# Chunk 1's keys moved into chunk 0's joins: a delta-rule attention and SiLU MLP kernel

## The chip, the cores and the metric

The kernel runs on one core of one Trainium2 chip. The metric is the device time of one execution in microseconds (us), taken as the median of several runs. Smaller is better. A profile of one execution, with its trace, goes with the runs.

## What is computed

Two blocks follow each other. The first is a delta-rule attention over 4 batches, 8 heads, 768 tokens and head size 48. Each head keeps a 48x48 state. The second block is a two-layer MLP on the attention's output, with 3072 tokens, 384 model features and 2048 hidden features.

```python
k_n = k / (np.linalg.norm(k, axis=-1, keepdims=True) + 1e-06)
for t in range(S):
    kt, vt, bt = (k_n[:, :, t], v[:, :, t], beta[:, :, t, None])
    y[:, :, t] = np.einsum('bhd,bhde->bhe', q[:, :, t], state)
    v_old = np.einsum('bhde,bhd->bhe', state, kt)
    state = state + bt[:, :, :, None] * np.einsum('bhd,bhe->bhde', kt, vt - v_old)
...
h = x @ w_in
g = h * (1.0 / (1.0 + np.exp(-h)))
return g @ w_out
```

Here x is y with its heads side by side. The attention's inputs are float32. The two weight matrices arrive in 64-bit floats and are narrowed to float32 on the chip.

## The kernel before

The 768 tokens are cut into 6 chunks of 128, and each chunk into two halves of 64. Chunk c is worked on for all 32 pairs of batch and head at once.

For the attention of a chunk the kernel does these things in turn. It loads keys, queries and values (`load_k`, `load_q`, `load_v`). It transposes them on the matmul engine (`turn`, L507) and copies them out with ScalarE or VectorE. It multiplies keys with keys and with queries (`score`, L536). Keys' own products go through DRAM (`block_out`, `block_in`), so that all 32x32 blocks lie side by side; VectorE then inverts them in 31 rank-one steps (`invert`, L643 and L648). The blocks are joined to the inverse of a half by small matmuls: in chunk 0 by four stages (`joins`: first, second, third, fourth, L746 to L787), in later chunks by `merge` (L821). With the inverse, `keys` (L846), `inner` (L858), `old` (L924), `update` (L878) and `new` (L937) carry the state from half to half and make the outputs. The outputs of even heads are copied into `xT` by ScalarE or VectorE (L551, L554), fourteen copies for a half; those of odd heads are copied as a whole (`part`) and then moved into `xT` by DMAs (`move`, L917).

The MLP of a half takes `hidden` (L1059: 8 pairs of feature tiles, which the text calls features 0 to 7, each in two steps of 3 matmuls, with a Silu on ScalarE at L1069 behind it) and then the second matrix: `project` (L1094) for both halves of chunk 0, `combine` (L1166) for all others. `hidden` of feature f reads piece f of `w_in`.

The weights come as eight pieces each of `w_in` and `w_out` (`fetch_w_in`, `fetch_w_out`). Each is narrowed (`narrow`) by two instructions on ScalarE (L224, L225), two on VectorE (L229, L233) and one on GpSimd (L237). `begin_next` issues the ScalarE part of the next piece, `fill` the rest in three steps.

Every engine takes its instructions in the order in which the program issues them; `pin` writes this order out. So does `in_line` for the DMAs that SyncE issues, and `linked` makes the next DMA wait until the one before it has landed. `busy` issues a matmul that only keeps the matmul engine at work.

The order around the change is written by hand. First comes straight code for chunk 0, up to the joins of its first half. Then a string of words is read by `script`: `s` is the next step of chunk 0's or 1's `solve`, `r` the next step of the MLP (`run`), `j` of the second half's joins, `p` of chunk 1's scores (`prepare`), `l` of chunk 1's and `m` of chunk 2's key lengths (`lengths`), `i` of the inversion of chunk 1's blocks, `f` and `b` are `fill` and `begin_next`, `q` turns a batch of chunk 1's queries, `g` makes the step sizes, `c` runs what is left of the MLP of chunk 0. A number behind a letter repeats the step.

Of the kernel before, what the change touches and what calls it, by code (L numbers as in the profile page):

```python
# [19 lines left out]
def kernel(  # L20
# [10 lines left out]
    nc = tc.nc  # L31
# [76 lines left out]
    def together(*parts):  # L108
        for _ in zip_longest(*parts):
            pass  # L110
# [109 lines left out]
    def narrow(to, raw):  # L220

        low, high = raw[..., 0], raw[..., 1]
        bits = to.bitcast(U32)
        pin(nc.scalar.activation(out=to, in_=high.bitcast(FP32), func=ACTF.Abs, scale=2.0**-112))  # L224
        pin(nc.scalar.activation(  # L225
            out=low.bitcast(I32), in_=low, func=ACTF.Identity, scale=2.0**-29, bias=plus23[:]
        ))
        yield
        yield pin(nc.vector.tensor_scalar(  # L229
            out=bits, in0=bits, scalar1=3, scalar2=0x7FFFFFFF,  # L230
            op0=ALU.logical_shift_left, op1=ALU.bitwise_and,
        ))
# [40 lines left out]

    def fetch_w_in(i):
        if i in (0, 1, 6):
            raw = mlp.tile([P, SIZE], U32, name="raw", tag="gT", bufs=3)[:]
# [100 lines left out]
    def square(c, b):  # L377

        if b == 0:
            sums[c] = small.tile([P, BH], FP32, name="ss", bufs=1)[:]  # L380
        if c > 2:
            squared[c, b] = zbuf[:, b].rearrange("p s a w -> p (s a) w")[:, :, 0:D]
        elif b % HB == 0:
            tag = "g" if c > 0 or b > 0 else "x"
            both = work.tile([P, HB, H, D], FP32, name="sq", tag=tag, bufs=1)
            for u in range(HB):
                squared[c, b + u] = both[:, u]
        kb = kbufs[c % 2][:, b].rearrange("p a e w -> p (a e) w")[:, :, 0:D]
        pin(nc.gpsimd.tensor_tensor(out=squared[c, b], in0=kb, in1=kb, op=ALU.mult))
# [168 lines left out]

    blocks = {}

    def dram_blocks(c):
        return tc.dram_tile([P, T, T], FP32, name=f"blocks{c}")

    def block_room(c):

# [18 lines left out]

    def block_out(c, g):

        there, ap = blocks[c][0], aps[c, g][0]
# [99 lines left out]
    def invert_first(step):  # L687
# [25 lines left out]
        def widen(to, of, q, by):  # L713
# [3 lines left out]
            else:  # L717
                pin(nc.vector.tensor_scalar(out=to, in0=of, scalar1=scale, scalar2=None, op0=ALU.mult))

        pin(nc.vector.transpose(  # L720
            out=turned[:, 0].rearrange("p n s -> p s n"), in_=x2.rearrange("p i s t -> p s i t")
        ))
        for q, by in enumerate(("dve", "dve", "act", "act")):
            widen(et, turned[:, 0], q, by)
        pin(nc.vector.transpose(
# [145 lines left out]
    def update(c, g, hf):  # L871

        if c == NCH - 1 and hf == 1:
            return
        pu = bank(CC, "pu")
        for u, p, e, n, of, _ in of_heads():
            rows = on(e, hf, g)
            yield pin(nc.tensor.matmul(  # L878
                pu[of, n * D : (n + 1) * D], lhsT=kbufs[c % 2][rows, g * HB + u, p, e, 0:D],
                rhs=zbuf[rows, g * HB + u, hf, p, 0:D], start=True, stop=True,  # L880
            ))
        to = states[g][:, :, :, 0:D]
        pin(nc.vector.tensor_tensor(out=to, in0=to, in1=by_heads(pu), op=ALU.add))
# [106 lines left out]
    def solve(c):  # L990

        if c == 0:
            together(inner(0, 0, 0, CC))
            together(inner(0, 1, 0, M))
            yield
            first_outputs(0)
            yield
            first_outputs(1)
            yield
            together(update(0, 0, 0), update(0, 1, 0))  # L1000
            yield
            together(keys(0, 0, 1), keys(0, 1, 1))
            yield
            together(inner(0, 0, 1), old(0, 0, 1))
            yield
            together(inner(0, 1, 1), old(0, 1, 1))
            yield
            together(update(0, 0, 1), update(0, 1, 1))
            yield
            together(new(0, 0, 1), new(0, 1, 1))  # L1010
            copy_out()
            copy_out()
            move()
            yield
            return
        together(merge(c, 0, False), merge(c, 1, False))
        yield
        together(keys(c, 0, 0), keys(c, 1, 0))
        yield
        together(merge(c, 0, True), merge(c, 1, True))  # L1020
        yield
        for hf in range(2):
            if hf == 1:
                together(keys(c, 0, 1), keys(c, 1, 1))
                if c > 1:
# [12 lines left out]
            move()  # L1038
            if hf == 0:
                yield  # L1040
# [192 lines left out]

    class Piece:
        def __init__(self, *name):
            self.name, self.steps, self.done = name, None, 0

        def begin(self):
            if self.steps is None:
                kind, i = self.name  # L1240
                self.steps = (narrow_w_in if kind == "in" else narrow_w_out)(i)
                next(self.steps)

    def begin(*names):
        for piece in queue:
# [7 lines left out]
            piece.begin()  # L1253
        soon.clear()

    def begin_next():
        for piece in queue:
            if piece.steps is None:
                piece.begin()
                return  # L1260

    def fill(n):
# [76 lines left out]
        pass  # L1339
    for g in range(2):  # L1340
        above_blocks(g)
    fetch_w_in(0)
    load_k(1)
    fetch_w_in(1)
    load_v(0)
    for c in range(1, NCH):
        beta_of(c)
    busy(1)
    for b in range(2, B):
        first_queries(b)  # L1350
        busy(1)
    linked(fetch_w_in, 2)
    linked(load_q, 1)
    fetch_w_in(3)
    linked(fetch_w_in, 4)
    linked(fetch_w_in, 5)
    linked(fetch_w_in, 6)
    begin(("in", 0))
    inv = invert_first(step)

# [5 lines left out]

    for n in range(1 + Q):
        done = next(inv)
        if n in (9, 11, 15, 16):
            busy(1 + n // 16, done, Sync)  # L1370
        if n in (10, 12):
            for b in range(n - 10, n - 8):
                turn(1, b, 0, M)
    stages = next(inv)

    def joins(hf, between=()):
# [15 lines left out]
    def none():  # L1392
        pass

    together(joins(0, [sized, none, none, filled(3)]))

    pieces = chained(hidden(0, 0), hidden(0, 1), project())

# [24 lines left out]
    def prepare(c):  # L1423
# [14 lines left out]
        if in_blocks(c):  # L1438
# [14 lines left out]
            block_in(c)  # L1453
            yield
            return
        block_room(1)
        for b in range(B):
            score(1, b, (0,), (CC, CC), evacuate)
            if b % HB == 1:
                block_out(1, b // HB)  # L1460
            yield
        block_in(1)
        yield
        for b in range(B):
# [13 lines left out]
    def script(text):  # L1478

        nonlocal pieces  # L1480
        for word in text.split():
# [18 lines left out]
                turn(1, queries_1.pop(0), 1, M)  # L1500
            elif what == "b":
                begin_next()
            elif what == "p":
                go(ready, n)
            elif what == "w":
# [24 lines left out]
                pieces = chained(feed_forward(1, 0), feed_forward(1, 1))  # L1530

    for text in (
        "s a a s q s b q f3 b j34 r f3 j34 r q f j34 r f2 q j38 W7 f r f b r f2 e r f h w2 f r l f s f l r2 w3 l p r l f p l s l f r l r l3 p l s l3 p l2 r l f l4 f l f l3 p l s l2 s2 f r v f r p l3 g i p f l p f i p f l i r3 i r i2 r3 i2 r i r i3 b r2 f2 r3 i r i2 r2 i f b i4 f r f r2 f r3 f i2 r f i f r3 f r f i f r i2 r i2 k i2 b r2 i r i r z r i r s r b z s b r2 t r2 f s r2 t2 m2 t2 b m f r m s f b r m r m2 b m f s r s m4 c s m7 r t s m r m5 s r m m t t",
    ):
        script(text)
    for c in range(1, NCH):
# [59 lines left out]
```

## Time and profile before

| | |
|---|---|
| median of 3 runs | 658.51 us (657.32 to 658.62) |
| profiled execution | 656.42 us, of which span 654.5 us |
| mean granted TensorE clock | 0.989 |
| TensorE matmuls (PE) busy | 630.7 us, 96% of the span |
| VectorE (DVE) busy | 395.6 us, 60% |
| ScalarE (ACT) busy | 218.9 us, 33% |
| GpSimd (POOL) busy | 89.6 us, 14% |

PE stands for TensorE's matmuls, DVE for VectorE, ACT for ScalarE, POOL for GpSimd and SP for SyncE. The profile divides the span in 40 slices of 16.4 us and gives the busy share of each engine in tenths. Its chain of waits goes back from the last instruction to what released each one. The trace also lists each engine's instructions in order of time: start in us, length in us, engine, line, operation, tiles, how often, and in brackets how long the engine was idle before and what ended it. L-numbers are lines of the kernel before.

### The profile page before, as it was taken

Reading aid. Unit: us, or ns where it says so; the run is one execution under the profiler, and the core shown is the slowest. Engines: PE = TensorE matmul, PEld = TensorE weight load, DVE = VectorE, ACT = ScalarE, POOL = GpSimd, SP = SyncE. Lnnn points to the kernel's source line nnn. Section 1 sums busy time; section 2 is a strip of 40 time slices with the busy share of each in tenths; the row PEclk is TensorE's granted clock in tenths of the full one; section 3 lists DMA queues with packets and bytes.
Section 4 is the critical chain, followed back from the end, with each engine's and each line's share of the span. In section 5 each row is a group of like instructions: output and inputs, shape, how many; then the busy total and the mean of one; then the engine's idle time right before and its main releaser. Section 6 shows DMA issues by size and latency. Waiting matters only on the chain.

```text
span 654.5 us, 20661 instructions
## 1 busy us (share of the span) xinstructions
PE 630.7 (96%) x9044; PEld 550.3 (84%) x9044; DVE 395.6 (60%) x895; ACT 218.9 (33%) x509; POOL 89.6 (14%) x94
## 2 busy tenths in 40 slices
PE   7799989999999999999999999999999999999997
PEld 5487778666789988989988989988989988889997
DVE  6846679988774985453986453986454974103112
ACT  2557763332351122451122451122451122441111
POOL 5023631335010020010020010020002000000000
PEclk9699999999999998999999999999999999999999
DMA  9976634350279333269325279325173023100101
GB/s 135 208 165 193 201 71 103 98 97 3 65 148 150 59 77 41 52 130 148 54 75 57 47 134 145 59 75 58 27 150 74 7 67 60 40 13 1 25 0 25
DMA packets 145673, 54.65 MB, mean 83 GB/s; under 512 B 117152, under 2 KB 138912, under 8 KB 145584
## 3 DMA queue, kind: packets, MB, share of 16 engines
q1 hardware_dynamic: 143136, 52.93, 41.0%
q8 instruction: 71, 1.16, 0.8%
q10 hardware_dynamic: 2448, 0.41, 0.4%
q14 instruction: 18, 0.15, 0.1%
HBM read 40.14 MB, written 11.01 MB: 78 GB/s over the span
## 4 chain that ended last, share of the span: by engine, by line
PE 66%; DVE 14%; DMA 9%; SPq 5%; ACT 2%; issue 2%; POOL 0%; POOLq 0%; DVEq 0%; ACTq 0%
PE phid L1059 22%; PE px L1166 11%; PE py L1166 8%; DVE rank L643 6%; PE po L1094 5%; DVE x L648 5%; PE pb_c L858 3%; DMA up<-x 2%; SPq L102 2%; DVE sums_of_g L1148 2%; PE pb_c L846 2%; DMA xe<-low 2%; PE pyc L937 2%; PE pa L536 2%; SPq L917 2%
## 5 line engine op out<-in xcount | busy, mean ns | idle before, releaser
L1059 PE MATMUL phid<-xT,w_in 128*128 128x256 f32 x1152 | 258.4, 382 | 2.7 <-DMA xT<-part 1.4
L1059 PEld LDWEIGHTS phid<-xT,w_in 128*128 128x128 f32 x1152 | 215.9, 190 | 34.9 <-issue 4.3
L1069 ACT ACTIVATE gT<-phid 128x512 f32<-128x512 f32 x88 | 52.5, 597 | 143.6 <-PE phid L1059 135.0
L643 DVE SCALAR_TENSOR_TENSOR rank<-g,step,x 128x31 f32<-128x31 f32 (+15 forms) x124 | 49.7, 401 | 39.1 <-DMA g<-blocks 35.7
L1148 DVE TENSOR_TENSOR sums_of_g<-gT 128x384 f32<-128x384 f32 (+1 forms) x60 | 31.2, 540 | 56.5 <-ACT gT L1069 45.9
L1166 PE MATMUL py<-w_out,sums_of_g 128*128 128x192 f32 x320 | 56.8, 329 | 0.0
L1166 PE MATMUL px<-sums_of_w,sums_of_g 128*128 128x192 f32 x320 | 56.8, 329 | 0.0
L1166 PEld LDWEIGHTS px<-sums_of_w,sums_of_g 128*128 128x128 f32 x320 | 52.2, 190 | 0.5
L1166 PEld LDWEIGHTS py<-w_out,sums_of_g 128*128 128x128 f32 x320 | 52.2, 190 | 0.4
L648 DVE TENSOR_TENSOR x<-x,rank 128x31 f32<-128x31 f32 (+15 forms) x124 | 42.5, 342 | 4.3
L474 POOL TENSOR_TENSOR vf<-vf,n_slot 128x768 f32<-128x768 f32 x10 | 15.0, 1516 | 173.6 <-DMA vf<-in_v_dram 126.0
L495 DVE STREAM_TRANSPOSE kq<-stage 128x512 f32<-128x512 f32 x28 | 28.4, 1110 | 10.6 <-DMA stage<-in_q_dram 10.1
L551 ACT COPY xT<-pyc 48x128 f32<-48x128 f32 (+2 forms) x126 | 32.6, 259 | 1.6
L1166 PE MATMUL px<-w_out,gT 128*128 128x192 f32 x160 | 29.7, 341 | 0.0
L1166 PEld LDWEIGHTS px<-w_out,gT 128*128 128x128 f32 x160 | 28.1, 200 | 0.5
L1166 PE MATMUL px<-sums_of_w,gT 128*128 128x192 f32 x160 | 28.4, 329 | 0.0
L1166 PE MATMUL py<-w_out,gT 128*128 128x192 f32 x160 | 28.4, 329 | 0.0
L1166 PEld LDWEIGHTS py<-w_out,gT 128*128 128x128 f32 x160 | 26.1, 190 | 0.3
L1166 PEld LDWEIGHTS px<-sums_of_w,gT 128*128 128x128 f32 x160 | 26.1, 190 | 0.2
L557 POOL COPY g<-x 64x256 f32<-64x256 f32 x4 | 5.0, 1244 | 154.5 <-DVE x L651 154.5
L1177 DVE TENSOR_TENSOR o<-o,kept 128x192 f32<-128x192 f32 (+1 forms) x29 | 11.4, 419 | 24.0 <-ACT kept L1174 24.0
L858 PEld LDWEIGHTS pb_c<-vf,xi 64*64 64x64 f32 x736 | 22.9, 135 | 3.5 <-issue 3.2
(228 smaller groups left out, 915.0 us busy)
## 6 DMA issues: line engine op xcount, KB each, us to landing
vf<-in_v_dram SPq DMA_DIRECT2D x48, 96.0 KB, 3.0
out_dram<-o SPq DMA_DIRECT2D x42, 96.0 KB, 2.2
w_out<-in_moe_w_in_dram SPq DMA_DIRECT2D x4, 768.0 KB, 4.6
sums_of_w<-in_moe_w_out_dram SPq DMA_DIRECT2D x4, 768.0 KB, 5.6
blocks<-ap SPq DMA_DIRECT2D x44, 64.0 KB, 2.1
g<-blocks SPq DMA_DIRECT2D x5, 512.0 KB, 3.7
kb<-in_k_dram SPq DMA_DIRECT2D x12, 192.0 KB, 4.9
kb<-in_k_dram SPq DMA_DIRECT2D x24, 96.0 KB, 4.3
```

What stands on the lines that cost most here:

```text
L102: in_line(nc.sync.dma_start(out=to, in_=of))
L474: pin(nc.gpsimd.tensor_tensor(out=vf, in0=vf, in1=of, op=ALU.mult))
L495: pin(nc.vector.transpose(out=kqs[c, b][:, :, j, :].rearrange("p a (i m) -> p a m i", i=T), in_=src.rearrange("p a (m d) -> p a m d", d=D) ...
L551: return pin(nc.scalar.copy(to, of))
L643: pin(nc.vector.scalar_tensor_tensor(out=tv, in0=g[:, 0:m, m : m + 1].to_broadcast([P, m, n]), scalar=step[:, m : m + 1], in1=x[:, m : m + ...
L648: yield pin(nc.vector.tensor_tensor(out=x[:, 0:m, m:T], in0=x[:, 0:m, m:T], in1=tv, op=ALU.add))
L858: yield pin(nc.tensor.matmul(pz[rows, n * D : (n + 1) * D], lhsT=xis[g][rows, u * H + 2 * p + e, :], rhs=vfs[c][rows, hf, g * HB + u, p, : ...
L1059: pin(nc.tensor.matmul(ph[:, j * GT : (j + 1) * GT], lhsT=w_in[:, a, (2 * f + j) * P : (2 * f + j + 1) * P], rhs=xTs[c, hf][:, a, :], star ...
L1069: pin(nc.scalar.activation(out=hidden_of(c, hf, f), in_=ph[:], func=ACTF.Silu, scale=-0.5 if in_blocks(c) else 0.5))
L1094: pin(nc.tensor.matmul(pos[i][:, 0:DM], lhsT=hidden_of(0, hf, f // 2)[:, at : at + C], rhs=w_outs[f // HFF][:, f % HFF, :], start=(f == 0) ...
L1148: pin(nc.vector.tensor_tensor(out=sums_of_g[:, k, fs], in0=of[0], in1=of[1], op=op))
L1166: pin(nc.tensor.matmul(to, lhsT=at, rhs=quarter(f, *b) if isinstance(b, tuple) else sums_of_w[b][:, f], start=start and f == 0, stop=f == ...
```

## The change

Nothing of the arithmetic changes; the order does, and with it some buffers.

- Chunk 1's keys are loaded ahead of piece 0 of `w_in` and turned right behind chunk 0's last query scores. Chunk 1's key scores (`prepare`, L1457) are issued between the stages of the second half's joins. The room of `block_room(1)` is taken only after them.
- The pieces 4 to 7 of `w_in` are fetched from the script (`L`, `W`), between chunk 1's block stores.
- The squares of chunk 1's keys are written to a part of `w_in` that is not narrowed yet, and not to a tile of their own.
- In chunk 0's `solve`, the state update of the second half comes after `new` and its copies.
- The two fillers between chunk 0's last query scores go; two are issued behind the turning of the inverted blocks, and the others wait for later steps of the inversion.
- The masks of chunk 0's query products are issued between the first half's joins, and half of piece 1's ScalarE work too: `narrow` can now stop between its two ScalarE instructions.
- The script's first part is new. From `b r2 f2 r3 i r i2 r2` on, its words are the old ones.

```diff
@@ narrow
         pin(nc.scalar.activation(out=to, in_=high.bitcast(FP32), func=ACTF.Abs, scale=2.0**-112))
+        yield
         pin(nc.scalar.activation(
...
@@ square
+        elif c == 1:
+            at = DFF - H * D * (1 + b // NKT)
+            squared[c, b] = w_in[:, b % NKT, at : at + H * D].rearrange("p (h d) -> p h d", d=D)
...
@@ invert_first
-        pin(nc.vector.transpose(
+        done = pin(nc.vector.transpose(
             out=turned[:, 0].rearrange("p n s -> p s n"), in_=x2.rearrange("p i s t -> p s i t")
         ))
+        busy(2, done, Sync)
...
@@ solve, c == 0
-            together(update(0, 0, 1), update(0, 1, 1))
-            yield
             together(new(0, 0, 1), new(0, 1, 1))
             copy_out()
             copy_out()
             move()
+            yield
+            together(update(0, 0, 1), update(0, 1, 1))
             yield
...
@@ begin_next
-    def begin_next():
+    def begin_next(n=2):
         for piece in queue:
-            if piece.steps is None:
-                piece.begin()
+            if piece.begun < n:
+                piece.begin(n)
                 return
...
@@ chunk 0
+    load_k(1)
     fetch_w_in(0)
-    load_k(1)
+    load_v(0)
     fetch_w_in(1)
-    load_v(0)
+    raw_6 = mlp.tile([P, SIZE], U32, name="raw", tag="gT", bufs=3)[:]
...
     for b in range(2, B):
         first_queries(b)
-        busy(1)
     linked(fetch_w_in, 2)
     linked(load_q, 1)
     fetch_w_in(3)
-    linked(fetch_w_in, 4)
-    linked(fetch_w_in, 5)
-    linked(fetch_w_in, 6)
+    for b in range(B):
+        turn(1, b, 0, M)
...
-        if n in (9, 11, 15, 16):
+        if n in (13, 14, 15, 16):
             busy(1 + n // 16, done, Sync)
-        if n in (10, 12):
-            for b in range(n - 10, n - 8):
-                turn(1, b, 0, M)
...
-    together(joins(0, [sized, none, none, filled(3)]))
+    def mask_and_fill():
+        masks(1, 1)
+        fill(3)
+
+    together(joins(0, [sized, lambda: masks(1, 0), none, mask_and_fill, none, lambda: begin_next(1)]))
...
@@ prepare
-        block_room(1)
         for b in range(B):
             score(1, b, (0,), (CC, CC), evacuate)
             if b % HB == 1:
                 block_out(1, b // HB)
             yield
+        block_room(1)
         block_in(1)
...
@@ script
+            elif what == "B":
+                begin_next(1)
+            elif what == "L":
+                linked(fetch_w_in, n)
...
-        "s a a s q s b q f3 b j34 r f3 j34 r q f j34 r f2 q j38 W7 f r f b r f2 e r f h w2 f r l f s f l r2 w3 l p r l f p l s l f r l r l3 p l s l3 p l2 r l f l4 f l f l3 p l s l2 s2 f r v f r p l3 g i p f l p f i p f l i r3 i r i2 r3 i2 r i r i3 b r2 f2 r3 i r i2 r2
+        "s b s s f3 r L4 b s r h j34 p r f3 l q j34 p L5 L6 r s b l r j34 p q r f3 l2 j38 p p r l3 b q s r l4 q W7 s f3 l6 r l5 b s v l4 l4 r e g f3 r i b r i f3 r w2 i b r i f3 r i w3 r i i f r2 p i f r2 i p f r2 i2 p r2 i r p r i s r i3 b r2 f2 r3 i r i2 r2
```

More of the change, by code (lines that the diff above doesn't have):

```diff
@@ L275, in fetch_w_in @@
         if i in (0, 1, 6):
-            raw = mlp.tile([P, SIZE], U32, name="raw", tag="gT", bufs=3)[:]
+            raw = raw_6 if i == 6 else mlp.tile([P, SIZE], U32, name="raw", tag="gT", bufs=3)[:]
         elif i < 6:
@@ L559 @@
     blocks = {}
+    in_dram = {}
     def dram_blocks(c):
-        return tc.dram_tile([P, T, T], FP32, name=f"blocks{c}")
+        if c not in in_dram:
+            in_dram[c] = tc.dram_tile([P, T, T], FP32, name=f"blocks{c}")
+        return in_dram[c]
     def block_room(c):
@@ L585, in block_out @@
     def block_out(c, g):
-        there, ap = blocks[c][0], aps[c, g][0]
+        there, ap = dram_blocks(c), aps[c, g][0]
         for j in range(NB):
@@ L1235, in __init__, with begin @@
         def __init__(self, *name):
-            self.name, self.steps, self.done = name, None, 0
-        def begin(self):
+            self.name, self.steps, self.done, self.begun = name, None, 0, 0
+        def begin(self, n=2):
             if self.steps is None:
@@ L1241, in begin @@
                 self.steps = (narrow_w_in if kind == "in" else narrow_w_out)(i)
+            while self.begun < n:
                 next(self.steps)
+                self.begun += 1
     def begin(*names):
@@ L1532 @@
     for text in (
-        "s a a s q s b q f3 b j34 r f3 j34 r q f j34 r f2 q j38 W7 f r f b r f2 e r f h w2 f r l f s f l r2 w3 l p r l f p l s l f r l r l3 p l s l3 p l2 r l f l4 f l f l3 p l s l2 s2 f r v f r p l3 g i p f l p f i p f l i r3 i r i2 r3 i2 r i r i3 b r2 f2 r3 i r i2 r2 i f b i4 f r f r2 f r3 f i2 r f i f r3 f r f i f r i2 r i2 k i2 b r2 i r i r z r i r s r b z s b r2 t r2 f s r2 t2 m2 t2 b m f r m s f b r m r m2 b m f s r s m4 c s m7 r t s m r m5 s r m m t t",
+        "s b s s f3 r L4 b s r h j34 p r f3 l q j34 p L5 L6 r s b l r j34 p q r f3 l2 j38 p p r l3 b q s r l4 q W7 s f3 l6 r l5 b s v l4 l4 r e g f3 r i b r i f3 r w2 i b r i f3 r i w3 r i i f r2 p i f r2 i p f r2 i2 p r2 i r p r i s r i3 b r2 f2 r3 i r i2 r2 i f b i4 f r f r2 f r3 f i2 r f i f r3 f r f i f r i2 r i2 k i2 b r2 i r i r z r i r s r b z s b r2 t r2 f s r2 t2 m2 t2 b m f r m s f b r m r m2 b m f s r s m4 c s m7 r t s m r m5 s r m m t t",
     ):
```

## The prediction

> **What bounds the kernel now.** I read the page first: its busy rows by slice, then its chain.
>
> ```profile
> PE   7799989999999999999999999999999999999997
> DVE  6846679988774985453986453986454974103112
> PEclk9699999999999998999999999999999999999999
> ```
>
> TensorE (PE) is busy almost everywhere from slice 3 on, and it works in program order, so the time is its fixed work plus its waits. The stages show where the waits lie: between 55 and 92 us PE is busy 34.1 of 37.0 us, from 100 to 171 us 70.8 of 71.0. Back to back, a hidden step (3 matmuls) takes 1.3 us (96 records of L1059 in 20.72 us), a projection matmul 0.645 us (6 records in 1.94 us). So a step moved ahead of 100 us gains only what waits it fills. Next the chain of waits, in order of time, cut to 160 to 262 us:
>
> ```profile
> 172.21 1.65 PE phid L1059 x6
> ...
> 180.53 4.61 DMA stage<-in_q_dram
> ...
> 238.59 4.08 DMA up<-x
> ...
> 243.09 3.42 DMA xe<-low
> ...
> 246.56 1.25 PE py L821 x80
> 247.81 4.48 PE px L1166 x16
> 252.29 1.08 PE pb_c L846 x64
> 253.36 2.80 PE px L1166 x16
> ```
>
> Here the path leaves PE: loads of chunk 2's queries, SyncE (SP) issues, blocks through DRAM, 31 rank steps on VectorE (DVE), DRAM again, merge. PE comes to that merge at 244.5 and waits in it until 246.6: only 2 us of slack. After that wait 16 records took 4.48 us instead of 2.80: the clock stood at 0.50 from 248 to 251. Where SP starts chunk 2's loads is thus worth as much as PE. SP's timeline there:
>
> ```profile
> 168.43 3.24 SPq L917 DMA_DIRECT2D xT<-part  x5
> 171.77 3.30 SPq L102 DMA_DIRECT2D out_dram<-o  x4
> 175.16 3.21 SPq L102 DMA_DIRECT2D out_dram<-kq  x4
> 178.47 6.54 SPq L158 DMA_DIRECT2D stage<-in_q_dram  x12
> ```
>
> The moves of chunk 1's outputs go first, chunk 0's eight stores behind them at 0.8 us each. Last, ScalarE (ACT) behind chunk 0's `new`, which ends on PE at 92.1:
>
> ```profile
> 92.23 0.58 ACT L551 COPY part<-pyc 48x512 f32<-48x512 f32 x1 [2.98 <-PE pyc L937]
> 92.83 1.61 ACT L551 COPY xT<-pyc 48x128 f32<-48x128 f32 x6
> 94.46 0.58 ACT L551 COPY part<-pyc 48x512 f32<-48x512 f32 x1
> 95.07 1.61 ACT L551 COPY xT<-pyc 48x128 f32<-48x128 f32 x6
> 96.70 0.60 ACT L1069 ACTIVATE gT<-phid 128x512 f32<-128x512 f32 x1
> 97.19 0.18 ACT L457 COPY step<-pg 128x32 f32<-128x32 f32 x1
> ```
>
> Fourteen copies in a row, 4.45 us, and whatever ACT has queued waits behind them.
>
> **Start (no gain).** SP issues chunk 1's keys ahead of w_in piece 0: six issues of 0.8 us or more from 17.5, then the piece, which I put at about 31 us landed; ACT wants it at 32.6, so that costs nothing up to 33.9 and a us for a us beyond. The two fillers between the query scores go, and 16 key transposes stand in their place; seven fillers then stand in one row before the joins (two of them wait for the turned blocks, done at 31.8). At the clock of that stretch (0.50 from 22.7 to 32.9) the transposes end about 31.8, the fillers take 1.36 us each cold and 0.65 warm: the first join starts at 37.0 instead of 37.23. Bounds: 35 if the clock rises one step sooner, 39 if one later.
>
> **Joins of the first half (2.3 us sooner).** Two query turns leave the place between the first outputs (PE 49.33 to 51.54, 52.4 to 53.0). Two mask instructions (0.69 us) enter DVE's queue, of which about 0.3 us meets the join copies. Hidden step 0 then waits for ACT: z copy to 49.9, the second half of piece 1 (1.0 us), two xT copies, DVE's add: 52.5 instead of 55.0.
>
> **Up to the end of `new` (8.4 us sooner, but with less done).** Before: 55.0 to 92.1, 37.1 us, of which 3.6 are waits (1.6 of them in the hidden steps at 66 to 73). After, by the program's order, 12 hidden matmuls (5.2) and the state update (0.9) are not yet done there, the second half's first join (2.0) and two turns (1.1) are: 30.6 us plus 0.5 for piece 4, so `new` ends at 83.7. That, not the 8.4 us, is to be compared: what is left for PE is larger.
>
> **Hidden steps behind `new` (7.4 us of new waits).** Features 5, 6 and 7 now stand behind `new`, and pieces 6 and 7 of w_in are narrowed behind ACT's fourteen copies: 83.8 plus 4.45, Silu 0.5, step size 0.2, L224 0.8: 89.8. DVE has its first two rank steps (1.0) ahead, then 0.69 and 0.96: 91.6; GpSimd (POOL) adds in 1.85 (L237 row): 93.5. Piece 5 comes at 87.6 (DVE's norm steps, blocked behind POOL's piece 4, stand ahead of it). Piece 7: DVE instructions are held while POOL works (102.01: 1.82 us for one of 0.25), so 93.5 plus four rank instructions 1.2, 1.6, 1.85: 98.1. Loads do not add to this: on SP the block stores of chunk 1 now stand between pieces 4, 5 and 6, each of which waits for the transfer before it, but by the page's 4.6 us from issue to landing they are there at about 74, 79 and 86, and ACT asks for them at 81, 89 and 91; with that cover of 5 us and more gone they would cost a us for a us. The four squares that POOL takes between pieces 2 and 3 (0.8 us each) lie in its idle time, 1.7 to 9 us ahead of each of pieces 0 to 4 before. PE has 9.55 us of work from 83.7 to the end of feature 7, and ends it at 100.7.
>
> **To the second keys of chunk 1 (+4.0).** From here PE is full in both. Before: hidden of the second half starts at 100.1, `keys` at 171.06, 70.9 us. After: 100.7 plus 70.9, plus four query scores (2.3), the update (0.8) and nine more changes between kinds of work at 0.1, less 0.5 of waits before the merge: 175.1. The inversion starts about 89 instead of 97.5, and the merge does not need it: PE reaches the merge at 154, the blocks are turned by about 150.
>
> **Chunk 1's first outputs (+4.9).** Six projection matmuls stood behind `new` (4.1 us) and hid ACT's copies and the moves. Now the projection ends before `update`, so the eight stores enter SP ahead of the five moves, and nothing is left on PE but `keys` (1.07). From the end of `new` the moved rows landed after 5.1 us before (167.0 to 172.1): at least 4.0 us of wait. With stores of 0.62 (226.42) to 0.82 us ahead it is 5.2 to 6.8; I take 6.0. A PE that idles so long restarts at half clock, as at 247.8; hidden step and `old` lose 2.3 us by the 1.7 us ratio of that row and the cold scores (1.06 against 0.63). `old` frees the query buffer: `stage` loads start at `keys` plus 1.07, 6.0, 1.65, 2.32, 2.3, 13.3 us, instead of 7.4: 5.9 later. PE itself comes to chunk 2's merge 7.4 later (8.3 less the 0.9 it waited for DVE at 186), so its wait there shrinks to 0.6; half of the cold 1.9 us behind it goes: 4.9.
>
> The Trainium skill, TensorE: Matmul & The Clock Gate, Part 1, says that activity is judged in free-running windows of 3.4 us and that one busy window lifts the throttle. By it a restart inside a window can stay cold for nearly two, an estimate of up to 3.4 us lost where the sum has 2.3, and the total would be 10.0; the trace agrees with the window at 248 to 251.3 and shows no restart of this kind.
>
> **Sum.** 4.0 and 4.9: 8.9 us. Against the profiled execution's own 656.42 that is 665.3; the median of the runs is 658.51, 2.1 above it, so 667.4.
>
> **Rivals.** *A, faster:* the front packs far better than I walked it. Place: 22.7 to the end of `new`; price: a us there is a us of the end; it decides from `new` at 74.8. For: between 37.2 and 55 PE has some 12.3 us of work in 17.8, with waits that no semaphore explains (0.79, 1.41), and 10 us of half clock. Against: all waits taken out, from a first join at 34.8, give 77.4. At 72 us the time is 655.7. Chance 0.11, and 0.03 for no difference (within 0.2%, 1.3 us, which is what a measurement of this kernel can tell). *B:* pieces 5 to 7 are ready, since ACT and POOL have idle time before `new`; against it stands ACT's order. Then 8.9 less 7.4: 660.0; 0.10. *C:* DVE becomes the bound at the merge. Some two and a half more narrowings (1.6 us and 1.5 of POOL's hold each) fall between its rank steps, and its masks wait in order for PE's query scores; it has 4 us to spare, beyond which each us counts: 8 us more of them give 671.4; 0.08. That the change does not do what it says is excluded: the order of the built program shows it.
>
> **How the numbers follow.** The forecast has 0.68, slower in all 0.86. Low: B's 660 with half a us: 659.5. High: `new` 2.5 later, the full store price, the longer cold spell and a part of C: 674.
>
> **Right or wrong.** The profile after would show `new` of chunk 0 ending near 84; PE gaps of 2 to 3 us before features 5, 6 and 7, ended by POOL; SP with `out_dram` rows ahead of the `xT` moves near 170; a PE gap of 5 to 7 us before chunk 1's first hidden step, and a low clock behind it; `stage` loads near 188. I am wrong if `new` ends before 78, if these features run without waits, or if that gap is under 4 us.

## The result

The changed kernel takes 682.17 us (median of 4 runs, 680.58 to 682.63) and the kernel before, on the same chip, 657.91 us. The ratio is 1.0372, with a 95% interval of 1.0337 to 1.0406. The forecast was 667.4 us with a range up to 674.0: slower was right, and the size was not; the loss is 24 us where 8.9 were worked out.

The profiled execution of the changed kernel took 681.77 us, with a span of 679.8 us and a mean granted clock of 0.970 (before: 656.42, 654.5 and 0.989). Lines of the code are 1 to 10 higher in it: `hidden` is L1069, `project` L1104, `merge` L831, `keys` L856, `new` L947, Silu L1079, the narrowing L224 to L238.

From the page, by slices of 17.0 us, as shown of before:

```profile
PE   8789969997879999999999999999999999999998
DVE  5854765894676498555498453797364893302112
PEclk9697989997979999999999999999999999999999
```

Slices are counted from 0. Before, PE was at 9 from slice 6 to the last but one, and the clock was below 9 in slices 1 and 15 alone. Now PE drops to 6 in slice 5 (85 to 102 us) and to 7, 8 and 7 in slices 9 to 11 (153 to 204 us), and the clock drops in slices 3, 5, 9 and 11. So these waits cost more than their own length: of the 25.3 us that the span grew by, 12.0 are idle time of PE, and 13.3 are longer busy time (630.7 to 644.0 us for the same 9044 matmuls). An estimate from the mean granted clocks, 0.030 of 679.8 us less 0.011 of 654.5, gives 13.2. The projection stage shows it best. First the kernel before, then the changed one; columns are the window, its length, busy time of PE, PEld, DVE, ACT and POOL with instruction counts, granted clock, DMA share, GB/s:

```profile
121.00:146.00 25.00, 24.96 (x106) 14.26 (x108) 23.74 (x35) 9.24 (x12) 8.80 (x6) 1.00 0.52 115
```

```profile
132.00:168.00 36.00, 31.71 (x90) 17.55 (x88) 27.79 (x37) 11.29 (x15) 14.17 (x9) 0.91 0.38 88
```

Before, PE works without a gap and at full clock. In the changed kernel 4.3 us are idle, and of the 31.7 busy ones a part ran at half clock. PE's timeline of the changed kernel names what it waited for (start, length, engine, line, tiles, count, idle time before):

```profile
157.59 0.81 PE L1104 MATMUL pb_c<-w_out,kq 128*128 128x384 f32 x2
162.65 2.93 PE L1104 MATMUL po<-w_out,gT 128*128 128x384 f32 x4 [4.25 <-POOL w_out L238]
165.37 1.49 PE L1104 MATMUL po<-w_out,kq 128*128 128x384 f32 x2
...
177.06 1.56 PE L1104 MATMUL po<-w_out,gT 128*128 128x384 f32 x4 [3.29 <-POOL w_out L238]
```

Two pieces of `w_out` (5 and 6) came too late. The chain of waits of the changed kernel tells what made them late; it answers to the chain from 160 to 262 us shown of before:

```profile
154.48 1.93 DVE up L632
...
157.63 0.87 DVE w_out L230
158.52 1.29 DVE w_out L234
159.81 0.94 issue
160.76 1.84 POOL w_out L238
162.65 4.21 PE po L1104 x6
...
175.36 1.66 DVE w_out L234
177.06 2.20 PE po L1104 x6
...
196.06 0.67 SPq L927
...
197.47 2.13 DMA xT<-part
199.73 2.35 PE phid L1069 x4
...
273.75 1.25 PE py L831 x80
275.00 2.80 PE px L1176 x16
```

VectorE first finishes the inversion (`up`, L632), copies it, and only then narrows piece 5; GpSimd adds, and PE goes on. Piece 6 (VectorE at 173.90, GpSimd at 174.99) stands behind the merge's copies in the same way; the row at 175.36 is piece 7's, beside GpSimd's work on piece 6. Below, the chain has the `xT` moves, as forecast; and the row behind chunk 2's merge is 2.80 us, where it was 4.48.

### The profile page after: what moved, and what is told of

It reads as the page before. It is cut to its first block, busy times and chain, and to the rows that moved or that the text cites. A ratio compares the mean times of both kernels' runs of the same rounds, so it can differ in the third digit from the quotient of the medians.

```text
span 679.8 us, 20650 instructions
## 1 busy us (share of the span) xinstructions
PE 644.0 (95%) x9044; PEld 557.1 (82%) x9044; DVE 394.4 (58%) x895; ACT 219.5 (32%) x509; POOL 88.0 (13%) x94
## 4 chain that ended last, share of the span: by engine, by line
PE 71%; DVE 15%; DMA 4%; SPq 3%; ACT 3%; issue 3%; POOL 1%; POOLq 0%; ACTq 0%; DVEq 0%
PE phid L1069 27%; PE px L1176 12%; PE py L1176 9%; DVE rank L652 5%; DVE x L657 3%; PE pb_c L868 3%; PE pa L540 3%; PE po L1104 2%; PE pyc L947 2%; PE pt L511 2%; DVE sums_of_w L657 2%; PE pb_c L856 2%; PE pb_c L353 2%; PE pb_c L888 2%; SPq L927 1%
## 5 line engine op out<-in xcount | busy, mean ns | idle before, releaser
L1069 PE MATMUL phid<-xT,w_in 128*128 128x256 f32 x1152 | 267.2, 389 | 11.2 <-POOL w_in L238 5.5
L1069 PEld LDWEIGHTS phid<-xT,w_in 128*128 128x128 f32 x1152 | 219.7, 194 | 46.3 <-issue 8.0
L1079 ACT ACTIVATE gT<-phid 128x512 f32<-128x512 f32 x88 | 52.4, 597 | 146.1 <-PE phid L1069 135.5
L1104 PE MATMUL po<-w_out,gT 128*128 128x384 f32 x64 | 25.3, 518 | 7.6 <-POOL w_out L238 7.5
L893 DVE TENSOR_TENSOR state<-state,pb_c 128x384 f32<-128x384 f32 x22 | 11.2, 550 | 31.8 <-PE pb_c L888 31.8
L1176 PE MATMUL px<-w_out,gT 128*128 128x192 f32 x160 | 28.0, 327 | 0.0
L1176 PEld LDWEIGHTS px<-w_out,gT 128*128 128x128 f32 x160 | 26.4, 190 | 0.5
```

Source lines behind the costliest of these rows:

```text
L1069: pin(nc.tensor.matmul(ph[:, j * GT : (j + 1) * GT], lhsT=w_in[:, a, (2 * f + j) * P : (2 * f + j + 1) * P], rhs=xTs[c, hf][:, a, :], star ...
L1079: pin(nc.scalar.activation(out=hidden_of(c, hf, f), in_=ph[:], func=ACTF.Silu, scale=-0.5 if in_blocks(c) else 0.5))
L1104: pin(nc.tensor.matmul(pos[i][:, 0:DM], lhsT=hidden_of(0, hf, f // 2)[:, at : at + C], rhs=w_outs[f // HFF][:, f % HFF, :], start=(f == 0) ...
L1176: pin(nc.tensor.matmul(to, lhsT=at, rhs=quarter(f, *b) if isinstance(b, tuple) else sums_of_w[b][:, f], start=start and f == 0, stop=f == ...
```

## The experiments

Each kernel was measured beside the kernel before. "Ratio" is against that kernel, with its 95% interval; the changed kernel has 1.0372. The intervals reach 2 to 5 us to either side, so differences of two or three us between variants rest on the traces. In the script's text an `f` is a third of a narrowing, an `r` a step of the MLP.

| run | median us | ratio |
|---|---|---|
| x1_fill | 671.40 | 1.0224 (1.0173 to 1.0274) |
| x2_steps | 673.49 | 1.0259 (1.0209 to 1.0308) |
| x3_moves | 684.31 | 1.0415 (1.0355 to 1.0474) |
| x4_front | 672.37 | 1.0237 (1.0187 to 1.0287) |
| x5_both | 666.49 | 1.0141 (1.0076 to 1.0207) |
| x6_silu | 670.74 | 1.0223 (1.0142 to 1.0303) |
| x7_warm | 669.65 | 1.0197 (1.0122 to 1.0271) |
| x8_cold | 669.11 | 1.0187 (1.0117 to 1.0256) |
| y2_update | 671.25 | 1.0227 (1.0160 to 1.0293) |
| y3_before_late | 664.78 | 1.0137 (1.0064 to 1.0210) |
| y4_before_steps | 664.97 | 1.0109 (1.0031 to 1.0188) |
| x5_all | 673.40 | 1.0259 (1.0183 to 1.0334) |
| z1_state | 669.19 | 1.0174 (1.0116 to 1.0231) |
| z2_state_front | 664.65 | 1.0105 (1.0060 to 1.0150) |
| z3_piece5 | 674.72 | 1.0253 (1.0206 to 1.0300) |

### Are the late pieces the cause? (x1_fill, z3_piece5)

x1 narrows two pieces of `w_out` more ahead of the inversion's end, and the last one ahead of the merge:

```diff
-... r f r i f r i2 r i2 k i2 b r2 i r i r z r i r s r b z s ...
+... r f r i f f6 r i2 r i2 k i2 b r2 i r i r z r i r f3 s r b z s ...
```

> Changed kernel, but the narrowing of w_out pieces 4 to 6 is issued earlier: six more fill steps between the late rank steps of chunk 1's inversion and three behind it, ahead of the merge. Everything else as in the changed kernel (682). Theory P (the projection waits for w_out pieces 5 and 6, whose VectorE part stands behind the inversion and behind the merge's copies): the two PE waits of 4.25 and 3.29 us and the half clock behind the first of them (about 3 us) go, 671 to 674. Rival M (the merge or what follows is late for a reason of its own, and the waits only cover it): the waits turn up at the merge or at chunk 1's first hidden step, within 2 us of 682.

It took 671.40 us. In its PE timeline the projection runs on into the merge without a gap, and the half-clock rows are gone:

```profile
157.53 1.45 PE L1104 MATMUL po<-w_out,gT 128*128 128x384 f32 x4
...
159.46 0.81 PE L1104 MATMUL pb_c<-w_out,kq 128*128 128x384 f32 x2
160.27 1.29 PE L831 MATMUL py<-xe_y,ap 32*32 32x32 f32 x128
```

Four records took 1.45 us here and 2.93 us in the changed kernel. The stage took 28.85 us (131.42 to 160.27) instead of 35.94. These 7.1 us are what the prediction lacked there. z3 gives only one piece (`f3` in place of `f6`, nothing ahead of the merge) and so takes the two waits apart:

> The changed kernel with one piece of w_out more (three fills) ahead of the inversion's end and nothing else. It separates the two waits of the projection: theory that piece 5 costs 4.25 us of wait and 3.3 of half clock, piece 6 its 3.3 us and some half clock: 673.5 to 675.5, the wait at 162 us gone and the one for piece 6 still there. Rival, VectorE or GpSimd turn the one into the other: 678 or more.

674.72 us, as the theory had it. Piece 5's wait is gone, piece 6's stands, with a part of the half clock behind it:

```profile
167.87 1.97 PE L1104 MATMUL po<-w_out,gT 128*128 128x384 f32 x4 [3.29 <-POOL w_out L238]
```

So piece 5 cost 7.5 us (682.2 to 674.7) and piece 6 some 3.3 (to 671.4); the intervals of z3 and x1 overlap, so the second rests on the trace more than on the medians.

### What made the pieces late? (y4_before_steps, y3_before_late)

At the merge the changed script has issued three steps of the projection more than the old one, and one narrowing less. A step is two matmuls, 1.36 us; the expectations below call the three steps three matmuls, and in truth they are the six that stood behind chunk 1's `new`. y4 moves them in the kernel before:

```diff
-... i3 b r2 f2 r3 i r i2 r2 ...
+... i3 b r2 f2 r6 i r i2 r2 ...
```

> The kernel before, with three projection matmuls moved ahead of the merge as in the changed kernel, all pieces narrowed where they were. Theory: only the cover of the wait for chunk 1's moved outputs is lost (2 us of 4.1), and piece 6 may be late by a us or two: 659 to 663 us. Rival, the moved matmuls already make the projection wait for its pieces as in the changed kernel: 666 us or more.

664.97 us: 7 us lost, nearer to the rival than to my figure, which took half the cover for the whole. The three moved steps alone make PE ask for piece 6 before VectorE has turned to it, and they take all the cover off the moved outputs:

```profile
162.22 2.93 PE L1094 MATMUL po<-w_out,gT 128*128 128x384 f32 x4 [3.30 <-POOL w_out L237]
...
185.15 1.19 PE L1059 MATMUL phid<-xT,w_in 128*128 128x256 f32 x2 [2.67 <-DVE n L422]
```

Before, neither wait was there: VectorE narrowed piece 6 at the same place in its order (150.86), and PE asked for it, by the program's order, only behind the second part of the merge (156.31). y3 also narrows one piece less ahead of the merge (three `f` taken out):

> The kernel before, with only the state of w_out's pieces that the changed kernel has at the merge: one piece less narrowed ahead of it and three projection matmuls more issued, nothing else of the change. Theory that this state alone makes the projection wait: PE waits of 3 us or more for pieces 5 and 6, ended by GpSimd, and some 10 us with the half clock behind them, on top of what the three moved matmuls cost by themselves (next run): 668 to 673 us. Rival, the projection waited in the changed kernel because its whole front was late: no such waits here, and within 3 us of the next run.

664.78 us, no different from y4: the theory missed, and the rival's number came out, though the wait for piece 6 (3.30 us) is there. The trace says why the run is no test of piece 5. In the kernel before the inversion is less far ahead in program order, so the forced narrowing of piece 5 fell ahead of the inversion's last transposes (L233 at 139.87, transposes from 140.74), and not behind them as in the changed kernel (158.52). The count of pieces was copied, the order was not. What speaks against the rival, that the whole front was late, is z3: it has the front of the changed kernel, and the wait for piece 5 is gone.

### Why does moving them back bring nothing? (x2_steps, x5_all, z1_state)

x2 is x1 with the three steps moved back (`r3` taken out of `b r2 f2 r3 i`).

> As x1_fill, and three MLP steps fewer are taken ahead of the merge, so that six projection matmuls stand behind chunk 1's first new again, as in the kernel before. Theory S (the missing cover and the eight stores ahead of the moves cost PE a wait of 4 us and a cold spell of about 3): 4 to 6 us less than x1_fill, 666 to 669. Rival (chunk 2's loads set the end there, and PE has room): within 1.5 us of x1_fill.

673.49 us, no gain on x1 and nearer to the rival. The wait for the moved outputs was gone, with the low clock behind it, but another had come ahead of it, at the merge:

```profile
161.47 1.56 PE L831 MATMUL py<-xe_y,ap 32*32 32x32 f32 x128 [3.82 <-DVE xe_y L630]
```

PE came to the merge at 157.65, ahead of VectorE, which had two narrowings more to do among its rank steps and waited 1.10 us for ScalarE's part of one. z1 therefore gives the changed kernel the pieces and steps that the kernel before has at the merge: piece 5 narrowed, 6 and 7 not (`f3` in place of `f6`, none ahead of the merge), and the three steps back.

> The changed kernel with the state at the merge that the kernel before has: piece 5 of w_out narrowed ahead of the inversion's end, pieces 6 and 7 behind the merge, three projection matmuls back behind chunk 1's `new`. Theory that VectorE, late by two more narrowings (3.4 us each with GpSimd's hold), took the gain of the second experiment (673.5) away at the merge: its wait of 3.8 us there shrinks to under 1.5, and with the matmuls as cover the time is 667 to 670, under the 671.4 of the fills alone. Rival, chunk 2's loads and its merge set the end and the cover is worth nothing: 671 to 673.

669.19 us, in the range of the theory. The merge waits 0.47 us for VectorE, piece 6 is not waited for, and the first hidden step behind `keys` loses 1.8 us to waits. Its interval and x1's overlap, so the trace carries this more than the time does. x5_all, with all fills, the earlier `w_in` pieces of the next section and the three steps back, showed the same wait of 3.83 us at the merge:

> Fills, earlier w_in pieces, and the three projection matmuls moved back behind `new` of chunk 1, all on the changed kernel. Theory that chunk 2's merge and VectorE at chunk 1's merge give the cover back, as in the second experiment: 665 to 668, no gain on the 666.5 of the two parts together. Rival, the matmuls bring what they hide (a wait of 2.8 us and a slow stretch of 1.5 to 3 us): 662 to 664. A version under 657 would need both that and the waits of features 6 and 7 gone, and is not expected.

673.40 us, above both ranges and worse than expected by 5. In its trace `new` ended at 93.5, in that of x5_both at 89.2, with the same instructions up to there; half-clock rows make the difference. Whether its other runs had them too is open.

### The waits behind chunk 0's `new` (x4_front, x5_both, z2_state_front)

x4 fetches pieces 4 to 6 of `w_in` together and narrows pieces 3 to 7 one slot earlier:

```diff
-... r L4 b s r h j34 p r f3 l q j34 p L5 L6 r s b l r j34 p q r f3 l2 j38 ...
+... r L4 L5 L6 b s r h j34 p r f3 l b q j34 p r s f3 l b r j34 p q r f3 l2 b j38 ...
```

> Changed kernel, but w_in pieces 5 and 6 are fetched ahead of chunk 1's block stores and pieces 3 to 7 are narrowed one slot of the order earlier, so that pieces 5 and 6 are done before chunk 0's new and piece 7 straight behind it; w_out piece 5 moves ahead of the end of the inversion by this too. Theory F (hidden features 5 to 7 wait for pieces 5 to 7 behind ScalarE's fourteen copies, 2.1, 3.4 and about 2 us, and a late w_out piece 0 holds the Silus for 1 to 2 more): 8 to 9 us less from the front, and the 4.25 us wait for w_out piece 5 goes in part, 667 to 673. Rival (VectorE or ScalarE is full in that stretch and the wait only moves ahead of new): 678 to 682.

672.37 us. Its waits in the front:

```profile
77.49 0.69 PE L540 MATMUL pb_c<-stage 48*64 48x64 f32 x30 [2.22 <-DVE xi L558]
...
94.58 2.83 PE L1069 MATMUL phid<-xT,w_in 128*128 128x256 f32 x12 [0.96 <-ACT step L461]
99.06 5.45 PE L1069 MATMUL phid<-xT,w_in 128*128 128x256 f32 x24 [1.66 <-POOL w_in L238]
```

The waits for features 5 to 7 shrink from 5.5 us to 2.6, and 24 records take 5.45 us instead of 8.47. A new wait of 2.2 us stands ahead of `new`, ended by VectorE, which now narrows there; one small instruction of it took 2.11 us beside GpSimd's work (74.87) where it takes 1.06 in the changed kernel (74.22). The edit also brings three `f` more ahead of the merge, so piece 5 is in time too (projection 28.78 us); the gain of 10 us is of both kinds. With x1's fills (x5_both):

> The fills of the first experiment and the earlier w_in pieces of the fourth, both at once, on the changed kernel; all turns and projection steps stay where they are. Theory that the pieces of the two weights were each late on their own (projection waits 10.5 us, waits of features 5 to 7 and of the Silu behind them some 5 to 6): the gains add but for the 2 us by which the earlier pieces held `new` up, so 4 us less than the 671.4 of the fills alone: 666 to 669, and no wait over 1 us on PE between 95 and 180 us. Rival, VectorE is the bound at the merge once PE comes there sooner: 670 to 672, with a wait of 2 us or more at the merge ended by VectorE.

666.49 us, in the range. The two edits bring 15.7 us together, where each alone brought 10.8 and 9.8, since both have piece 5 in time. Not as expected, waits of 1.67 us (to 98.97) and 1.01 us (to 109.46) are left. And with the state at the merge of z1 instead of the fills:

> As the run before it, with the earlier w_in pieces of the fourth experiment. Theory: 662 to 665, a further 5 us less by the waits behind `new` of chunk 0. Rival, the earlier pieces put half-clock spells into the front, as in the run with all three parts (673.4): 667 or more, with `new` of chunk 0 behind 90 us.

664.65 us, in the range, and a ratio of 1.0105, the best order found of the changed kernel; none beat the kernel before. In its PE timeline the moved outputs are no longer waited for:

```profile
176.44 0.81 PE L1104 MATMUL pb_c<-w_out,kq 128*128 128x384 f32 x2
177.17 1.15 PE L856 MATMUL pb_c<-state,stage 48*64 48x48 f32 x64
178.25 1.72 PE L1069 MATMUL phid<-xT,w_in 128*128 128x256 f32 x6
```

The second keys start 6.1 us later than before (171.06), and up to 104 us its PE still waits 8.3 us in six places (2.31, 1.66, 1.42, 1.28, 0.95, 0.69).

### Smaller terms (x6_silu, y2_update, x7_warm, x8_cold, x3_moves)

x6 is x1 with one `f` put two hidden steps later (`i i f r2 p i f r2` becomes `i i r2 p i f2 r2`), which was meant to hold back the first instruction of `w_out` piece 0.

> The fills of the first experiment, and the first instruction of w_out's piece 0 put two hidden steps later, so that ScalarE does not stand in front of its load with PE's Silus behind it. If that load holds the Silus: the PE wait of 2.0 us at 106 us ended by ScalarE goes and the time is 669 to 670 instead of 671.4. Rival, something else is as late there (piece 7 itself, or VectorE at the merge): wait moves to the next instruction, 671 to 672.

670.74 us. The edit did not do what the expectation says. In the trace ScalarE's two instructions of piece 0 (102.54, 103.36) still stand ahead of both Silus (104.24); only piece 1's came later (108.26, where x1 has 106.56). `new` to the first query score took 22.1 us instead of 23.4, but because the load of piece 0 was quicker. It stands in the chain of waits of x1, and of x6:

```profile
97.92 6.02 DMA w_out<-in_moe_w_out_dram
```

```profile
97.80 4.72 DMA w_out<-in_moe_w_out_dram
```

The changed kernel, without any edit there, took 22.1 us too. So x6 is no test of its theory.

y2 is x1 with the state update ahead of `new` again:

> The fills of the first experiment on the changed kernel, and one part of the change undone: the state update stands ahead of chunk 0's `new` again. Theory that the update's 0.8 us of PE work only changes places and PE waits for w_in's pieces behind `new` in either order: `new` 0.8 us later, the pieces with it, the later slot 0.9 shorter, 670.5 to 672.5 (671.4 with the fills alone). Rival, the later `new` costs in full: 673 or more.

671.25 us, as expected: what this part of the change costs, if anything, is too little for these runs to tell.

x7 is x1 with `busy(2)` behind each of chunk 0's first outputs:

> The fills of the first experiment, and two filler matmuls behind each of chunk 0's first outputs, where two query turns stood before the change. If the wait for the copies there and the half clock behind it cost `new` its 2 to 4 us: `new` of chunk 0 ends 1.5 to 3 us sooner than its 85.7 in the first experiment, the time is 669 to 670. Rival, the fillers only take the place of the wait and their own time is lost: `new` within 0.7 us, 671 to 672.

669.65 us. The first hidden step took 1.42 us instead of 2.83 and the update 0.86 instead of 1.46; `new` ended 47.7 us after the first join began, against 49.9, 48.4 and 48.9 in x1, z3 and x8, which have the same front, and 50.5 in the changed kernel. So the half clock costs 2.0 us in these two steps, of which the fillers give back a part: `new` came 0.7 to 2.8 us sooner, where the others differ by 2.1 among themselves. The medians do not tell x7 from x1.

x8 is x1 with `busy(4)` behind chunk 1's second keys:

> The fills of the first experiment, and four filler matmuls (2.6 us at full clock) behind chunk 1's second keys, in the wait for the moved outputs. If the low clock after that wait costs hidden step, `inner` and `old` their 3 us (3.74 instead of 1.65, 3.30 instead of 2.32): those come back to 1.7 and 2.4 and the time is 668.5 to 669.5 instead of 671.4. Rival, chunk 2's loads through SP set the end anyway, or the slow steps wait for later moves: 671 to 672, with the time given back as a longer wait at chunk 2's merge.

669.11 us, not told from x1. The fillers themselves ran at half clock but for the first two records (six in 3.81 us):

```profile
189.05 3.81 PE L353 MATMUL pb_c<-state,ident 128*128 128x384 f32 x6 [0.33 <-DVE vf L861]
192.65 1.59 PE L1071 MATMUL phid<-xT,w_in 128*128 128x256 f32 x6
```

The hidden step came back to 1.59 us and `inner` with `old` to 2.40, but the step began 7.95 us after `keys` did, and in x1 PE took up the last two records of the step 8.16 us after it (190.10), when the last move, issued at 188.0 and 1.9 us in landing, was there. So x1's slow hidden step (3.74 us) is mostly the wait for the last of five moves. From `keys` to the update 0.7 us were won (13.4 against 14.1 us). The rival holds for the most part.

x3 holds chunk 0's eight stores until the moves of chunk 1 are issued:

```diff
-                    store(0, hf, to, n)
+                    held.append((0, hf, to, n))
...
             move()
+            release()
```

> Changed kernel, but chunk 0's eight stores are issued behind the moves of chunk 1's first outputs, and not ahead of them. If the stores ahead of the moves are the price, as the prediction had it, PE's wait at chunk 1's first hidden step falls from 5.3 us to about 3.5, and the end comes 1.5 to 3 us sooner, 679 to 680.5. If the missing matmuls behind new are the price and SyncE's sum of issues stays, the loads of chunk 2's queries start no sooner and the end stays within 1 us of 682.

684.31 us, above both ranges. The gap behind `keys` shrank (3.24 us from `keys` to the hidden step instead of 5.26), but the `stage` loads then stood behind the stores, at 206.64, 11.0 us after `keys`, where they start 10.2 after it in the changed kernel. The issues that stand ahead of these loads on SyncE are the same in sum, and putting the moves first brought nothing.

## Why the prediction was wrong

Each step against the changed kernel's trace; the last column is what the step itself added:

| point | forecast | measured | added |
|---|---|---|---|
| `new` of chunk 0 ends | 83.7 | 87.6 | 3.9 |
| hidden of the second half starts | 100.7 | 106.9 | 2.3 |
| PE starts chunk 1's merge | 154 | 168.1 | 7.8 |
| second keys of chunk 1 | 175.1 | 193.0 | 3.9 |
| end, against before | 8.9 | 25.3 | -1.5 |

The added ones sum to 16.4 us, the error of the forecast against the profiled execution.

**The start** was right: the first join began at 37.14 (forecast 37.0).

**Joins and `new`.** Hidden step 0 began at 53.40 (52.5), behind two waits for copies of 1.42 and 1.28 us. I had let the two query turns go at no price, though they covered just these copies; behind the waits the first hidden step took 2.83 us. The granted clock from 54 to 84 us was 0.91, which is 2.7 us of 30 (0.50 from 53 to 56, 0.57 from 56 to 60, 1.00 from there on). This is a term of the sum that was mis-sized, by 3.9 us.

**Features 5 to 7** went as worked out: piece by piece 3.9, 9.8 and 14.4 us behind the end of `new`; in the trace PE resumed 3.8 and 10.1 us behind it, and GpSimd finished piece 7 at 102.0, 14.4 behind it. What I missed came next. ScalarE's timeline, which answers to the fourteen copies shown of before:

```profile
90.57 1.61 ACT L555 COPY xT<-pyc 48x128 f32<-48x128 f32 x6
92.21 0.60 ACT L1079 ACTIVATE gT<-phid 128x512 f32<-128x512 f32 x1
...
104.64 0.90 ACT L224 ACTIVATE w_out<-w_out 128x768 f32<-128x768 f32 x1 [7.92 <-DMA w_out<-in_moe_w_out_dram]
...
106.31 1.07 ACT L1079 ACTIVATE gT<-phid 128x512 f32<-128x512 f32 x2
```

Two Silus that PE needs stand behind L224, which waits for the load of `w_out` piece 0. SyncE issued that load at 99.88, behind chunk 0's moves and eight loads of values:

```profile
94.03 5.75 SPq L189 DMA_DIRECT2D vf<-in_v_dram  x8
99.88 1.14 SPq L296 DMA_DIRECT2D w_out<-in_moe_w_out_dram  x2
```

"Loads do not add to this" was weighed for `w_in` alone. No run was made to move this load, but its own spread tells what it is worth. In the eight profiled executions with this order (the changed kernel, x1, x2, x3, x6, x8, z1, z3) it took 4.5 to 6.3 us in the chain, and PE went on 19.1 to 20.9 us behind `new`, later by a us for a us: 4.52 and 19.1 in z3, 4.73 and 19.3 in the changed kernel, 6.02 and 20.6 in x1, 6.30 and 20.9 in z1. The half clock that PE shows from 97.7 to 103.8 us is covered by this wait: z3 ran at full clock there, waited 1.49 us more for GpSimd and 1.84 us for the Silu, and went on only 0.2 us sooner.

**"From here PE is full in both"** is the step that failed, with 7.8 of the 16.4 us. It took the projection of before, back to back, and moved it; it did not ask when the pieces that it reads are narrowed. Piece 5 cost 4.25 us of wait, and 2.7 us more, since the eight matmuls behind it took 5.41 us (162.65 to 168.06) where x1 takes 2.74. x1 and z3 show it by taking it away. Piece 6 cost 3.3. "The merge does not need" the inversion was right for the merge and wrong for what stands behind it on VectorE: piece 5. The prediction saw that the six matmuls had left their place behind chunk 1's `new`, and priced only the cover that they took along; y4 shows that they also bring a wait for piece 6 where they go.

**Chunk 1's first outputs** went as described, at a smaller price. SyncE's timeline, answering to 168.43 to 178.47 of before:

```profile
189.90 2.50 SPq L102 DMA_DIRECT2D out_dram<-o  x4
192.50 3.46 SPq L102 DMA_DIRECT2D out_dram<-kq  x4
196.06 3.31 SPq L927 DMA_DIRECT2D xT<-part  x5
...
203.16 2.75 SPq L158 DMA_DIRECT2D stage<-in_q_dram  x6
```

The stores are ahead of the moves, and the moves are issued 3.0 us after `keys` began. The gap was 4.2 us (forecast 6.0, bound 4.0), `hidden` and `old` behind it lost 3.4 us (2.3). The `stage` loads came 10.2 us after `keys` instead of 13.3. Chunk 2's merge waited 0.5 us (0.6), and the whole credit of 1.7 us behind it came, not half. Tail: 3.4 us against 4.9.

**Rivals.** A (the front packs better) and B (pieces 5 to 7 ready) did not happen; x4 and z2 show that B can be had in part by another order. A's 12.3 us of work between 37.2 and 55 us is too little: by the profile of before PE is busy 15.3 of these 17.8 us. C, VectorE as the bound at the merge, does not show at the merge of the changed kernel, where VectorE idles 9.02 us for PE ahead of its copies; but its inversion is in the chain just ahead (154.48), by way of piece 5, which C did not name. At the merge it came at once when PE was no longer held up: 3.82 us in x2, 3.83 in x5_all.

Of what is left in z2 (1.0105, or 6 us by the medians and 8.3 by the profiled executions), 5.7 us lie ahead of the projection (126.5 against 120.8 before); of what they consist was not taken apart further.

## What to carry to other kernels

When a step is moved up in an in-order queue, its operands' due times move with it: look up, for each operand, which instruction makes it and what stands ahead of that one on its engine, and do so also for the steps that only slide up because another one left. An engine with idle time in the profile can still be late with one piece, if the piece stands behind a chain that has to finish first. Giving the pieces earlier can cost as much as it brings, if the engine that makes them is next to become the bound: x2 narrows two pieces more ahead of the merge than z1 does and took 673.49 us against 669.19, and PE's wait for VectorE at the merge is 3.82 us in it against 0.47. When an edit is meant to move an instruction, look in the trace whether that one has moved: x6 gave a shorter time for another reason.

## What the runs showed of the hardware

How long the clock stays low after a wait does not follow from the wait's length. PE's granted clock in the changed kernel (windows as above, the clock third from the end):

```profile
162.00:164.00 2.00, 1.35 (x2) 0.84 (x3) 0.00 (x0) 0.00 (x0) 2.00 (x2) 0.50 0.00 0
166.00:168.00 2.00, 2.00 (x4) 0.67 (x2) 0.00 (x0) 0.00 (x0) 0.00 (x0) 0.50 0.00 0
168.00:170.00 2.00, 2.00 (x131) 1.76 (x131) 0.35 (x1) 0.39 (x1) 0.00 (x0) 0.83 0.03 8
...
174.00:177.00 3.00, 0.00 (x0) 0.00 (x0) 2.96 (x3) 0.00 (x0) 2.01 (x1) 1.00 0.00 0
177.00:179.00 2.00, 1.94 (x6) 1.25 (x7) 1.70 (x2) 0.00 (x0) 1.04 (x2) 1.00 0.00 0
```

After the wait of 4.25 us PE worked from 162.65 to about 168.7 at 0.50: 6.0 us, 3.0 of them lost. After the wait of 3.29 us the clock never fell. In y4 a wait of 3.30 us left four records at 2.93 us, in the changed kernel one of 3.29 us left four at 1.56. In all, the same four records took 1.56 us (the changed kernel, y3), 1.64 (x4), 1.97 (z3), 2.20 (x3) and 2.93 (y4) behind waits of 3.28 to 3.30 us. So a wait of this length costs up to 1.4 us more in these records alone, or nothing, and its length does not tell which.

The Trainium skill, TensorE: Matmul & The Clock Gate, Part 1, has the clock judged in free-running windows of 3.4 us. Windows that fall differently in each execution would fit these rows; no run here sets where they fall. The Trainium skill's sentence there that whatever is issued in the first 3.4 us runs slow falls short of them: 6.0 us here. The prediction's estimate from it, up to 3.4 us lost at a restart, holds the 3.0; it does not hold the next one, from 198.27 to 206.2 us at 0.50, with a gap of 0.3 us inside: 7.9 us, an estimated 3.8 lost. The stretch of before that the prediction names, 22.7 to 32.9 us at 0.50, is longer still, with PE busy 8.8 of its 10.2 us.

The first join began between 35.7 and 39.3 us in the profiled executions, though the programs up to there are the same in all variants of the changed kernel (35.7 to 37.4 in these, 36.5 to 39.3 in the variants of before). A us at one point of one trace is thus no evidence by itself here. Nor is a stretch between two points, unless the difference is beyond the spread of kernels with the same order there: `new` to the first query score took 21.9 to 25.4 us in the eight named above.
